# A transformer block's backward pass in head halves: column passes, a fixed TensorE order and dx in two buffers

## The chip, the cores and the metric

The kernel runs on one core of one Trainium2 chip. The metric is device time in microseconds (us) of one launch. It computes the forward pass and all gradients of one block in a single launch.

TensorE (PE) multiplies: a stationary operand is loaded into its array (the weights), a moving operand streams past, and the result lands in PSUM. VectorE (DVE), ScalarE (ACT) and GpSimd (POOL) work on rows; POOL and SyncE (SP) also issue the DMA transfers of this kernel. Each engine works through its own instruction queue in order and waits for others through semaphores.

## The reference

A block with a memory-augmented recurrent attention and a gated feed-forward layer, and the gradients of everything for a given `grad_out`:

```python
def _A_ref(x, mem0, Wq, Wk, Wv, Wo, seg_len):
    ...
    mem = mem0
    for s in range(n_seg):
        xs = x[:, s * seg_len:(s + 1) * seg_len, :].copy()
        h = jnp.concatenate([mem, xs], axis=1)
        q = jnp.einsum('btd,dhe->bhte', h, Wq)
        k = jnp.einsum('btd,dhe->bhte', h, Wk)
        v = jnp.einsum('btd,dhe->bhte', h, Wv)
        scores = jnp.einsum('bhqe,bhke->bhqk', q, k) * scale
        scores = jnp.where(mask[None, None], scores, -1000000000.0)
        p = _softmax(scores, axis=-1)
        o = jnp.einsum('bhqk,bhke->bhqe', p, v)
        o = jnp.einsum('bhte,hed->btd', o, Wo)
        mem = o[:, :M, :].copy()
        outs.append(o[:, M:, :])
    return jnp.concatenate(outs, axis=1)
...
h = x + _A_ref(_layernorm(x, axis=-1), A_mem0, A_Wq, A_Wk, A_Wv, A_Wo, A_seg_len)
h2 = h + _B_ref(_layernorm(h, axis=-1), B_w_gate, B_w_up, B_w_down)
...
_out, _vjp = jax.vjp(_f, A_x, A_mem0, A_Wq, A_Wk, A_Wv, A_Wo, B_w_gate, B_w_up, B_w_down)
_grads = _vjp(grad_out)
```

The sizes are: 2048 tokens of width 448; 16 heads of 256, so 4096 columns of q, k and v; segments of 32 tokens with 8 memory rows ahead of them, so 40 rows to a segment and 64 segments. The memory of a segment is the attention output of the first 8 rows of the segment before it. So the segments are a chain: forward from the first to the last, and backward from the last to the first, where what comes back to the memory rows of segment s is part of the output gradient of segment s-1. The feed-forward layer has an inner width of 1792. Inputs and outputs are bfloat16.

## The kernel before, in words

The launch has four stages, one after the other in time: the forward chain (0 to about 1045 us), the feed-forward layer with its gradients (1045 to 1356), the backward chain (1358 to about 2417) and the tail, which makes the weight gradients (2430 to the end).

A width of 448 is held as four chunks of 128 rows, the last half filled (`KC` = 4). The 4096 columns are 32 chunks of 128 (`MC`). On-chip memory is laid out by hand in three arenas, `arW`, `arA` and `arB`; PSUM has five banks named `psf`, two named `fx` and one named `po`.

**Order of work.** The program is written as a sequence, and a scheduler puts each engine's instructions in order by readiness and urgency: what stands under `k.prio.crit()` (the chain) goes first, and other work fills in where the chain waits. `tc.issue_after(x)` keeps an instruction behind x in its engine's order.

**Forward chain, what the change touches.** A tile of the output of earlier segments is fetched again (`fetch`, lines 604 and 605: two POOL loads) and added to the input (`residual`, L595 and the statistics after it on DVE). At segment s, with `jm` = s % 16, a fetch is issued where `jm % 3 == 1` and a residual where `jm % 3 == 0 and jm > 0`. The forward makes q and k rows by column passes (`qk_rows`, L535 and L539): the 32 new rows of a segment are the stationary operand, at four column positions of the array, and 512 columns of the weights stream past each.

**Feed-forward.** At its end each tile of the gradient `dh` is written twice to memory: in float32 (`DH`) and in bfloat16, padded from 448 to 512 columns (`DHb`, L1021 and L1022). The padding is zero.

**Backward chain.** The loop runs over s from 63 to 0; a tile t is four segments, r = s % 4 going 3, 2, 1, 0. `do_roll` holds the output gradient of the segments, transposed: per segment 32 columns of data and 8 of memory, with room for 8 segments. One segment is:

- L1151: the gradient ahead of the output projection, 128 products with a 128x128 block of `WoT_sb` as stationary operand and the 40 columns of the segment moving. Four banks of eight chunks; DVE and ACT copy them to `doT` (feature-major).
- `token_major`, L1160 and L1161: sixteen transposes and two ACT copies give `dO_sb`, token-major.
- L1169: `doT` times v, the gradient of the probabilities, 32 products into one bank `pD`. L1176, L1178, L1179 and L1181 on DVE make the gradient of the scores of all heads, written with zero blocks between head groups (`dS_bd`) by means of `P_bd`, the probabilities with zero blocks.
- `heads` (L1128 is its product): v from `dO_sb` and `P_bd`, k from q and `dS_bd`, q from k and the turned scores `dST_bd` (L1209). Sixteen products of 80 columns each; copies to `blk` (the 32 rows of a segment's data) and to `lo` (its 8 memory rows) on DVE and ACT.
- `rows_in`, L1200: 96 products over the chunks of v, k and q with `WvT_sb`, `WkT_sb` and `WqT_sb`, collected in `po`. This is the gradient of the layer's normalised rows.
- L1218 and L1219 copy it to `om`; L1222, four float32 products with a selection matrix, turns it; L1226 (DVE) writes 8 columns into `do_roll` of segment s-1. That closes the chain: L1151 of the next segment needs it. The other 24 columns of each group go to `dxT`.

Once a tile, outside of the urgent part: L1264, 96 products of the memory rows (`lo`) of the four segments with the same weights, collected in a bank `fx` (px); then L1267, L1271, the copies into `dxT`, four transposes (L1279), the layer-norm backward (`ln_bwd`) and the store of the gradient of x (`OUT1`). L1264's products are used where the chain leaves TensorE free.

On POOL's queue per segment: the load of the probabilities (L1082), two copies into `P_bd` (L1084), a copy of memory gradients (L1239) and, at set places (`later`, `stores`), the stores of q, k and v gradients (L1247, L1251). On SP's queue: the loads of v, q and k, and per tile of `xn_t` and `dh_h`.

**Tail.** `d_by_e` collects seven banks over blocks of rows, with the 64-row chunk (L1380) after every four blocks. `rows_by_d` (L1396) collects n banks over blocks, block by block, then copies and stores them. The last product group multiplies the feed-forward activations (`Zt`) by `grad_out` (`GO`, loaded at L1471) and stores the 14 results of `OUT[9]` from POOL (L1479).

## Time and profile before

| | us |
|---|---|
| median of 3 runs | 3105.77 |
| lowest and highest | 3103.6, 3115.08 |
| the profiled execution | 3105.46 |
| its span | 3103.7 |
| mean granted TensorE clock | 0.988 |

The stages, from the busy time of each engine in each stretch of the same execution (us):

| stretch | length | PE | DVE | ACT | POOL | DMA share |
|---|---|---|---|---|---|---|
| 0 to 1045, forward | 1045.0 | 936.8 | 536.0 | 435.2 | 255.8 | 0.65 |
| 1045 to 1356, feed-forward | 311.0 | 305.5 | 214.2 | 150.1 | 91.9 | 0.96 |
| 1358.4 to 2417, backward | 1058.6 | 1010.6 | 497.1 | 432.1 | 210.4 | 0.52 |
| 2430 to 3103, tail | 673.0 | 658.9 | 81.9 | 92.2 | 115.9 | 0.81 |

A line of a timeline has the start in us, the length in us, the engine, the line of the program, the operation, its output and inputs with the arrays' names, the shape, and after "x" how many such instructions were put together. In brackets stands how long the engine was idle just before, and what released it. In a line of the page's groups, the two figures after the bar are the busy time in us and the mean length of one instruction in ns, and after the second bar the idle time before them.

### The profile page before, as it was taken

How to read it: one execution, taken by the hardware profiler on the slowest of the kernel's cores; microseconds unless marked ns; L12 is line 12 of the kernel's file. 1: busy time of each engine (PE TensorE's matmuls, PEld its weight loads, DVE VectorE, ACT ScalarE, POOL GpSimd, SP SyncE). 2: the span in 40 equal slices, each digit the busy share in tenths (PEclk: the TensorE clock that was granted, in tenths of full speed). 3: DMA queues.
4: the chain of work that ended last, by engine and by line, in shares of the span. 5: the costliest groups of instructions: out<-in, count | busy, mean ns of one | idle time of the engine just before them, and what ended most of it. 6: DMA issues, size and time to landing. Idle time of an engine off the chain costs nothing.

```text
span 3103.7 us, 108341 instructions
## 1 busy us (share of the span) xinstructions
PE 2914.8 (94%) x47640; PEld 1735.5 (56%) x47650; DVE 1331.6 (43%) x3381; ACT 1112.6 (36%) x2634; POOL 674.7 (22%) x1511
## 2 busy tenths in 40 slices
PE   5899999989988999989999999999999899999998
PEld 3555555545544555666666666666666454444443
DVE  3555455455455576654444444544445101111110
ACT  2444344344444544443434344444344001111110
POOL 2222222222222222321122111221211111212111
PEclk9999999999999999999999999999999899999999
DMA  6567756756756899984455445555544999969951
GB/s 242 136 172 178 183 162 167 191 158 167 189 161 182 276 222 228 221 298 119 133 150 143 128 137 142 143 139 136 141 138 133 284 267 244 190 181 199 192 160 57
DMA packets 739084, 550.12 MB, mean 177 GB/s; under 512 B 600052, under 2 KB 634852, under 8 KB 736180
## 3 DMA queue, kind: packets, MB, share of 16 engines
q1 hardware_dynamic: 687380, 389.19, 51.5%
q0 software_dynamic: 51232, 154.00, 14.9%
q8 instruction: 374, 6.13, 0.8%
q14 instruction: 98, 0.80, 0.1%
HBM read 168.01 MB, written 234.23 MB: 130 GB/s over the span
## 4 chain that ended last, share of the span: by engine, by line
PE 72%; issue 11%; DVE 6%; DMA 5%; ACT 4%; POOL 2%; SPq 1%; ACTq 0%; POOLq 0%; DVEq 0%
PE po L1200 7%; PE psf L1151 7%; PE psf L535 6%; PE psf L652 5%; PE po L697 4%; PE psf L1375 4%; PE psf L890 4%; PE psf L1128 4%; PE psf L1396 4%; PE fx L1264 3%; PE fx L1014 3%; PE fx L464 2%; PE psf L1222 2%; DVE arA L75 2%; PE psf L549 2%
## 5 line engine op out<-in xcount | busy, mean ns | idle before, releaser
L75 DVE CAST arA<-psf 128x256 bf16<-128x256 f32 (+3 forms) x933 | 427.2, 480 | 808.6 <-PE psf L1375 275.2
L76 ACT CAST arA<-psf 128x96 bf16<-128x96 f32 (+5 forms) x915 | 352.4, 409 | 1036.6 <-PE psf L1375 261.2
L1200 PE MATMUL po<-arW,arA 128*32 128x448 bf16 x6144 | 347.3, 355 | 4.6 <-DMA arW<-Tq 3.5
L1375 PE MATMUL psf<-arW,arA 128*128 128x512 bf16 x980 | 247.1, 380 | 0.0
L1375 PEld LDWEIGHTS <-arA 128*128 128x128 bf16 x1440 | 136.0, 98 | 164.8 <-issue 13.8
L1151 PEld LDWEIGHTS <-arW 128*128 128x128 bf16 x8192 | 213.4, 96 | 25.0 <-issue 25.0
L1151 PE MATMUL psf<-arA,arW 128*128 128x40 bf16 x8192 | 217.0, 180 | 6.2 <-DVE arA L1226 5.1
L652 PE MATMUL psf<-arW,arA 128*64 128x512 bf16 x1536 | 219.0, 386 | 0.0
L1200 PEld LDWEIGHTS <-arA 128*32 128x32 bf16 x6144 | 152.0, 96 | 115.8 <-ACT arA L76 9.4
L535 PE MATMUL psf<-arW,arA 128*32 128x512 bf16 x3072 | 193.8, 385 | 12.5 <-DVE arA L738 12.5
L76 ACT CAST arB<-psf 128x64 bf16<-128x64 f32 (+3 forms) x384 | 121.8, 318 | 153.1 <-PE psf L539 109.7
L697 PE MATMUL po<-arW,arA 128*32 128x256 bf16 (+1 forms) x4096 | 144.2, 267 | 10.5 <-DVE arA L75 7.5
L890 PE MATMUL psf<-arW 128*128 128x256 bf16 (+1 forms) x1288 | 146.3, 274 | 1.3 <-DVE arA L956 0.7
L890 PEld LDWEIGHTS <-arW 128*128 128x128 bf16 (+1 forms) x1344 | 102.4, 97 | 51.4 <-issue 40.8
L1161 ACT COPY arA<-psf 128x1024 bf16<-128x1024 bf16 x128 | 123.3, 1015 | 2.2 <-PE psf L1160 0.4
L1128 PEld LDWEIGHTS <-arW 128*128 128x128 bf16 x2048 | 86.4, 99 | 61.8 <-issue 56.9
L535 PEld LDWEIGHTS <-arA 128*32 128x32 bf16 x3072 | 70.6, 97 | 90.0 <-DVE arA L738 18.1
L76 ACT COPY arA<-psf 128x512 bf16<-128x512 bf16 (+3 forms) x142 | 84.3, 594 | 99.9 <-DVE arA L75 90.3
L464 PE MATMUL fx<-arA,arW 128*128 128x64 bf16 (+1 forms) x2048 | 84.3, 196 | 32.4 <-ACT arB L76 19.2
L697 PEld LDWEIGHTS <-arA 128*32 128x32 bf16 x4096 | 95.9, 98 | 32.9 <-DVE arA L75 10.5
L1128 PE MATMUL psf<-arB,arW 128*128 128x80 bf16 x2048 | 96.8, 201 | 13.6 <-DVE arB L1181 5.2
L1436 POOL DMA_DIRECT2D out_dram<-arA x96 | 51.7, 546 | 249.7 <-DVE arA L75 246.9
(290 smaller groups left out, 4645.7 us busy)
## 6 DMA issues: line engine op xcount, KB each, us to landing
arW<-T SPq DMA_DIRECT2D x256, 128.0 KB
X_o<-arA SPq DMA_DIRECT2D x37, 512.0 KB
T<-arA SPq DMA_DIRECT2D x64, 256.0 KB
X_v<-arA POOLq DMA_DIRECT2D x32, 512.0 KB, 4.9
X_k<-arA POOLq DMA_DIRECT2D x32, 512.0 KB, 4.0
X_q<-arA POOLq DMA_DIRECT2D x32, 512.0 KB, 3.1
out_dram<-arA POOLq DMA_DIRECT2D x90, 128.0 KB, 3.5
VG<-arA SPq DMA_DIRECT2D x64, 160.0 KB
```

The source lines that it names most:

```text
L75: return nc.vector.tensor_copy(out=out, in_=in_)
L76: return nc.scalar.copy(out=out, in_=in_)
L464: nc.tensor.matmul(banks[w][:, i * 64:(i + 1) * 64], lhsT=lhsT, rhs=xr[lo:hi, kc, :], start=(kc == 0 and i == 0), stop=(kc == KC - 1), ski ...
L535: nc.tensor.matmul(banks[w][32 * q:32 * q + 32, :], lhsT=hT_roll[:, kc, sl, M:L], rhs=(Wq_sb, Wk_sb)[w][:, kc, col(q, b)], start=(kc == 0) ...
L652: nc.tensor.matmul(pV[b][64 * g:64 * g + 64, 0:512], lhsT=hT_flat[:, kc, sl * L:sl * L + 64], rhs=Wv_sb[:, kc, n * 512:(n + 1) * 512], sta ...
L697: nc.tensor.matmul(pO[32 * q:32 * q + 32, 0:w], lhsT=xblk[:, j, r * SEG:(r + 1) * SEG], rhs=Wo_sb[:, cj(j), 256 * dh:256 * dh + w], start= ...
L890: nc.tensor.matmul(ps[fp][:, f2 * 256:(f2 + 1) * 256], lhsT=Wt[lo:hi, kc, c * P:(c + 1) * P], rhs=xT[lo:hi, kc, :], start=(kc == 0 and f2 ...
L1128: nc.tensor.matmul(ps[b][:, i * 2 * L:(i + 1) * 2 * L], lhsT=lhs[:, at, :], rhs=rhs_bd[:, cl // 2, :, :].rearrange("p g n -> p (g n)"), st ...
L1151: nc.tensor.matmul(pss[b][:, jj * L:(jj + 1) * L], lhsT=WoT_sb[:, kc, c * P:(c + 1) * P], rhs=do_roll[:, kc, sl, :], start=(kc == 0), stop ...
L1200: nc.tensor.matmul(pH[32 * (j % 4):32 * (j % 4) + 32, 0:D], lhsT=blk[nm][:, j, r * SEG:(r + 1) * SEG], rhs=WT[:, cj(j), :], start=(nm == " ...
L1375: nc.tensor.matmul(pa[2 * kc + g][:, 0:w], lhsT=lhs_of(b)[:, kc * P:(kc + 1) * P], rhs=rhs_of(b, g), start=(b == 0), stop=(b == nblk - 1), ...
L1396: k.last_mm = nc.tensor.matmul(pa[i][:, 0:D], lhsT=lhs_of(b, i), rhs=rhs_of(b), start=(bi == 0), stop=(bi == len(nblk) - 1))
```

## The change

- **Forward:** the fetch needs `jm > 3` as well, the residual `jm > 5`.
- **Feed-forward:** the padding of `DHb` repeats the last 64 columns instead of zeros.
- **Backward, TensorE in program order:** every product and transpose of the stage is issued through `in_order`, behind the one before it. Nothing of the stage can be moved up into a gap any more.
- **Column passes:** `wide_pass` takes the 32 non-memory rows (the columns 8 to 40 of a segment in `do_roll`: 24 of its data and the 8 of memory) as the stationary operand at four column positions and streams the columns of Wo past: 32 products of 512 columns into two banks. These give the token-major `dO_sb` at once; `half_turned` makes `doT` from it by eight transposes in two halves. The first 8 rows of each segment of a tile are done once a tile in the same way (`rest_pass`, `dO_rest`), turned into `R`, and copied by POOL into `doT` per segment. Wo's last 64 rows are held in `WoT3`, doubled.
- **v heads:** replaced by `values`, 16 products of 160 columns: eight for the main rows and eight for the first 8 rows, with the probabilities in two new layouts. `Pq_main` is loaded per segment by four DMAs (`load_p_main`); `Pq_rest` is made by DVE (`rest_probs`) from `Pr`, which 16 DMAs load per tile (`load_p_rest`), and a mask. `P_bd` and its copies are gone.
- **Head halves:** the gradient of the scores, the k and q heads and the turned scores are done in two halves of heads, with `rows_in` between them. All copies of v are on ACT.
- **Memory-row products:** the L1264 products become `px_part` (32 at a time: q at r = 0, k at r = 3 and v at r = 2 of the next tile) and `px_end` at r = 1, each whole at the end of a segment ahead of the last copies; `dx_end` follows at r = 0. `dxT` has two buffers.
- **Tail:** the 64-row chunk can be done at the end of a group (`frees=False`); `rows_by_d` does its last four blocks accumulator by accumulator; `GO` is loaded earlier, to another place; the last stores alternate between POOL and SP.

The core of the diff:

```diff
-        if due and jm % 3 == 1:
+        if due and jm % 3 == 1 and jm > 3:
             fetch(due[0], h_t, x2_t)
...
-        if due and jm % 3 == 0 and jm > 0:
+        if due and jm % 3 == 0 and jm > 5:
             n = due.pop(0)
...
             nc.scalar.copy(out=dh_b[:, 0:D], in_=dh_t)
+            nc.scalar.copy(out=dh_b[:, D:DP], in_=dh_t[:, D - 64:D])
...
+    def in_order(op):
+        def fn(*args, **kw):
+            with tc.issue_after((pe[0] if pe else k.last_dh).ins):
+                pe[:] = [op(*args, **kw)]
+            return pe[0]
+        return fn
+    mm, tr = in_order(nc.tensor.matmul), in_order(nc.tensor.transpose)
...
-        for g in range(2):
-            pool_op = nc.gpsimd.tensor_copy(out=P_bd[64 * g:64 * g + L, :, g, :], in_=P_sb[64 * g:64 * g + L, :, :])
...
+    def load_p_main(s):
+        for q in range(4):
+            g, x = divmod(q, 2)
+            src = dr["P_all"][s, 64 * g + M:64 * g + L].rearrange("i (b x h n) -> i b x h n", b=2, x=2, n=L)
+            nc.gpsimd.dma_start(out=Pq_main[32 * q:32 * q + 32].rearrange("p (b h) q n -> p b h q n", b=2)[:, :, :, 2 * x + g, :],
+                                in_=src[:, :, x])
+
+    def load_p_rest(t):
...
+        for q in range(4):
+            g, x = divmod(q, 2)
+            for i in range(4):
+                src = dr["P_all"][4 * t + i, 64 * g:64 * g + M].rearrange("i (b x n) -> i b x n", b=2, x=2)
+                nc.gpsimd.dma_start(out=Pr[32 * q + M * i:32 * q + M * i + M].rearrange("p (b h) n -> p b (h n)", b=2), in_=src[:, :, x])
...
+    def wide_pass(banks, out, lhs_of):
+        for q in range(4):
+            for b in range(2):
+                mm(banks[b][32 * q:32 * q + 32, :], lhsT=lhs_of(KC - 1, 64 * b, 64 * b + 64),
+                   rhs=WoT3[64 * b:64 * b + 64, q * 512:(q + 1) * 512], start=True, stop=False, skip_group_check=True)
+        for b in range(2):
+            for kc in range(KC - 1):
+                for q in range(4):
+                    mm(banks[b][32 * q:32 * q + 32, :], lhsT=lhs_of(kc, 0, P), rhs=WoT_sb[:, kc, col(q, b)],
+                       start=False, stop=(kc == KC - 2), skip_group_check=True)
+        for b in range(2):
+            k.evac(out[:, b, :], banks[b][:], "vs"[b])
+
+    def half_turned(pt, src, dst, b):
+        for i in range(4):
+            tr(pt[:, (4 * b + i) * P:(4 * b + i + 1) * P], src[:, b, i * P:(i + 1) * P], ident[:, :])
+        k.evac(dst[:, 16 * b:16 * b + 16], pt[:, 512 * b:512 * b + 512].rearrange("p (c n) -> p c n", n=32), "vs"[b])
...
+    def rest_pass():
+        wide_pass([k.fx1(), k.fx1()], dO_rest, lambda kc, lo, hi: hR[lo:hi, kc].rearrange("p g i -> p (g i)"))
+
+    def rest_probs(s):
+        with tc.issue_after(k.last_ds.ins) if s < NSEG - 1 else nullcontext():
+            nc.vector.tensor_tensor(out=Pq_rest, in0=Pr.unsqueeze(2).to_broadcast([P, 4, 4, L]),
+                                in1=gmask[:, s % 4, :].unsqueeze(1).unsqueeze(3).to_broadcast([P, 4, 4, L]), op=ALU.mult)
...
+        load_p(s - 1)
+        if r == 0:
+            load_p_rest(t - 1)
+        pool_op = nc.gpsimd.tensor_copy(out=doT[:, :, 0:M], in_=R[:, :, M * r:M * r + M])
+        stores("mid", s, pool_op.ins)
...
+            wide_pass([k.ps1(), k.ps1()], dO_sb, lambda kc, lo, hi: do_roll[lo:hi, kc, sl, M:L])
...
+            half_turned(pt, dO_sb, doT[:, :, M:L], 0)
+            pv += [k.ps1() for _ in range(3)]
+            values(1)
+            half_turned(pt, dO_sb, doT[:, :, M:L], 1)
             pD = k.ps1()
...
+            grad_of_probs(0)
+            grad_of_scores(0)
+            values(0)
+            if s > 0:
+                load_p_main(s - 1)
+            grad_of_probs(1)
+            grad_of_scores(1)
...
+            if r == 0 and t < NT - 1:
+                dx_end(t + 1)
+            rows_in("v", WvT_sb, 0, 12)
+            heads("k", Q_sb, dS_bd, 0)
+            turned_scores(0)
+            rows_in("v", WvT_sb, 12, MC)
+            if r == 0 and t > 0:
+                rest_pass()
+            heads("k", Q_sb, dS_bd, 1)
+            turned_scores(1)
+            heads("q", K_sb, dST_bd, 0)
+            rows_in("k", WkT_sb, 0, 12)
+            heads("q", K_sb, dST_bd, 1)
+            rows_in("k", WkT_sb, 12, MC)
+            if r == 0 and t > 0:
+                wide_turned(dO_rest, R)
+            if s > 0:
+                rest_probs(s - 1)
             rows_in("q", WqT_sb, 0, MC)
+            if r == 0:
+                px_part(t, "q")
+            elif t < NT - 1:
+                {3: lambda: px_part(t + 1, "k"), 2: lambda: px_part(t + 1, "v"), 1: lambda: px_end(t + 1)}[r]()
...
-            for b in range(b0, min(nblk, b0 + 4)):
+            for b in range(b0, min(nblk, b0 + 4)) if frees else range(nblk) if b0 + 4 >= nblk else ():
...
-        for bi, b in enumerate(nblk):
-            for i in range(n):
-                k.last_mm = nc.tensor.matmul(pa[i][:, 0:D], lhsT=lhs_of(b, i), rhs=rhs_of(b), start=(bi == 0), stop=(bi == len(nblk) - 1))
+        m = len(nblk) - 4
+        for bi, i in [(bi, i) for bi in range(m) for i in range(n)] + [(bi, i) for i in range(n) for bi in range(m, m + 4)]:
+            b = nblk[bi]
+            k.last_mm = nc.tensor.matmul(pa[i][:, 0:D], lhsT=lhs_of(b, i), rhs=rhs_of(b), start=(bi == 0), stop=(bi == m + 3))
```

## The prediction

> **What bounds the kernel now.** I read the page's busy shares and its chain first, then the timeline of one steady backward segment, then the three places that the change touches outside it. TensorE (PE) is busy 94% of the span, and the chain lies on it for 72%:
>
> ```profile
> PE 2914.8 (94%) x47640; PEld 1735.5 (56%) x47650; DVE 1331.6 (43%) x3381; ACT 1112.6 (36%) x2634; POOL 674.7 (22%) x1511
> PE 72%; issue 11%; DVE 6%; DMA 5%; ACT 4%; POOL 2%; SPq 1%; ACTq 0%; POOLq 0%; DVEq 0%
> L1200 PE MATMUL po<-arW,arA 128*32 128x448 bf16 x6144 | 347.3, 355 | 4.6 <-DMA arW<-Tq 3.5
> L1151 PE MATMUL psf<-arA,arW 128*128 128x40 bf16 x8192 | 217.0, 180 | 6.2 <-DVE arA L1226 5.1
> ```
>
> The backward chain runs from 1358.4 to about 2417. The starts of L1151 give its segment periods: 16.04, 16.04, 16.90, 15.98 in an undisturbed tile of four (64.95), 65.2 as a mean, 24.73 and 17.15 in the first two segments. One segment on PE (start, length, idle before in brackets):
>
> ```profile
> 1708.63 3.37 PE L1151 MATMUL psf<-arA,arW 128*128 128x40 bf16 x128
> 1711.84 1.12 PE L1160 MATMUL psf<-ident,arA 128*128 128x128 bf16 x16
> 1712.89 0.69 PE L1169 MATMUL psf<-arA 128*64 128x40 bf16 x32
> 1713.61 0.46 PE L1128 MATMUL psf<-arB,arA 128*128 128x80 bf16 x8
> 1714.00 0.56 PE L1264 MATMUL fx<-arW,arA 128*32 128x448 bf16 x8
> ...
> 1723.40 0.85 PE L1222 MATMUL psf<-sel,omb 128*128 128x32 f32 x6
> 1724.18 0.55 PE L1264 MATMUL fx<-arW,arA 128*32 128x448 bf16 x5
> 1724.67 0.49 PE L1151 MATMUL psf<-arA,arW 128*128 128x40 bf16 x13
> ```
>
> No bracket shows: whenever the chain waits, L1264 (memory-row products, of low urgency) fills. Adding start-to-start times, the chain's own matmuls are 12.9 us and the 37 L1264 1.74; 1.4 of the 16.04 goes to switches and short waits. Meanwhile VectorE (DVE) has slack; its softmax gradient, with the four durations that I use:
>
> ```profile
> 1713.63 0.49 DVE L1176 SCALAR_TENSOR_TENSOR prod<-psf,arB 128x320 f32<-128x320 f32 x1 [1.91 <-PE psf L1169]
> 1714.51 0.48 DVE L1178 TENSOR_REDUCE rsum<-prod 128x8 f32<-128x320 f32 x1
> 1715.36 0.48 DVE L1179 SCALAR_TENSOR_TENSOR prod<-psf,rsum 128x320 f32<-128x320 f32 x1
> 1715.95 0.82 DVE L1181 TENSOR_TENSOR arB<-prod,arB 128x640 bf16<-128x640 f32 x1
> ```
>
> **The Trainium skill.** "TensorE: Matmul & The Clock Gate", Back-to-back issue gap, puts an issue floor of about 25 ns under small matmuls. The trace agrees: 128 L1151 start over 3.21 us, 25 ns each, for only 40 columns; so fewer, wider products pay. "TensorEngine Tiling (Array Packing)", PSUM Bottleneck, warns that after packing the PSUM copies may become the bottleneck; before, they are not (DVE 7.2, ACT 6.0 busy of the 16.04), and this is my main doubt after. "PSUM — Partial Sum Buffer", PSUM bank collisions raise a hardware error, tells to guard by bank, not by address: so two halves in one bank wait for each other's reader. No run shown here has such a wait inside a segment. The clock gate page's part on HAM says that idleness of a window drops the clock to half; after the 6.4 us stall below the granted clock reads 0.50 from 625 to 632.
>
> **The change part by part.**
>
> **Forward.** Segments 20, 36 and 52 take 19.86, 24.54, 20.54 against 15.07 for the next:
>
> ```profile
> 623.04 0.39 DVE L595 TENSOR_TENSOR arB<-arB 128x448 bf16<-128x448 bf16 x1 [6.70 <-DMA arB<-in_A_x_dram]
> ...
> 625.09 0.46 PE L628 MATMUL psf<-arA 128*40 128x40 bf16 x16 [6.41 <-ACT arA L76]
> ```
>
> L595 sits in DVE's queue ahead of copies that the chain needs. In the changed instruction order each L595 comes about three segments after its fetch. Next late is the normal period: −(4.8+9.4+5.4) = −19 us; −12 if the wait only shrinks.
>
> **Feed-forward.** Sixteen ACT copies of 64 columns (0.2 each) replace memsets, with ACT half idle there (150 busy of 311): 0; uncovered 3.
>
> **Backward, work on PE.** Out: L1151 3.21, L1160 1.05, the v heads 0.66 = 4.9 us a segment. In: the column pass, the same 24 + 8 shapes as a forward unit:
>
> ```profile
> 380.09 1.48 PE L535 MATMUL psf<-arW,arA 128*32 128x512 bf16 x24 [0.27 <-DVE arA L738]
> 381.50 0.41 PE L539 MATMUL psf<-arW,arA 64*32 64x512 bf16 x8
> 381.83 1.04 PE L535 MATMUL psf<-arW,arA 128*32 128x512 bf16 x14
> ```
>
> that is 1.74; eight transposes 0.46; sixteen values products of 160 columns, 0.08 each by estimate between the 80-column heads (41 ns) and 448-column rows (190 ns alone), 1.28; a fifth product at the end 0.15. Sum 3.6. Once a tile, the rest pass and its transposes add 2.2. Net per tile 4×(3.6−4.9)+2.2 = −3.0 us of work.
>
> **Backward, waits.** L1264 no longer fills: its products stand as whole chunks at the segment's end. I laid one segment out with the traced durations, a handover 0.05, a switch of shape 0.1: column pass 0–1.74; its bank copied by DVE (0.69), transposes to 2.17; memory-row values to 2.85; second transposes 3.09; first half of L1169's product 3.12, whose last matmul reads past its half and waits for ACT's 0.59 copy, 3.94; rest of the values 4.56. The second half writes the bank that DVE still reads: three 160-column operations (0.32 each, the forward's softmax row) end at 5.23, so PE waits 0.7. Then 5.64; v rows to 6.21; k heads and turned scores 6.83; v rows 7.78; second k heads wait for DVE's other half (7.86), done 8.66; q heads 9.00; k rows 9.57; second q heads wait for ACT's copy (9.9), 10.28; k rows 11.23; q rows 12.74; a chunk of 32 L1264 14.25; the fp32 products 15.5; DVE's copy 15.8. Period 15.85. DVE's gradient as two halves is 2×5×0.32 = 3.2 where it was 2.3, and the new rest probabilities add the 0.82 of L1181's shape.
>
> With r=1 the 32-product chunk (1.51) gives way to 8 fp32 products (1.09): 15.4. With r=0 come the rest pass 2.2, four transposes 0.65, their switches 0.5, and 0.5 as the rest pass's second product waits for DVE's layer-norm step in the same bank: 19.7. Tile: 15.85+15.85+15.4+19.7 = 66.8 against 65.2, +1.6, times 16 = +26 us. Bounds: if waits cost no more than the 1.4 of today, 14.6+14.6+14.15+17.9 = 61.25, −3.95×16 = −63; above, rival B. I take the laid-out order, since each of its waits is a fixed place in an in-order queue.
>
> **Backward, DMAs.** Per segment POOL issues four more loads, minus two copies of 0.465; per tile 16 small loads at 0.54 (L1082's row), 8.6 us. They stand ahead of the copy that puts memory rows into doT, and are moved past that copy's readers. They can start when the last rest probabilities of the tile are made (8.84 in the r=1 segment), so the copy ends at 8.84+8.6+0.54+0.5 = 18.5, which is 3.1 in the next segment; it is needed at 3.12. Taken as hidden, just. SP's queue gets the dx loads a segment later; they are needed two segments on: 0.
>
> **Start of backward.** Those 16 loads, four wide ones and the copy now precede the first segment's product (16+4)×0.54 = 10.8 us behind the last feed-forward stores, and the rest pass 2.2; some lies beside the 9 us of waits that the first segment has. I take +12 (5 to 20).
>
> **Tail.** grad_out is loaded earlier:
>
> ```profile
> 3048.19 2.03 PE L1396 MATMUL psf<-arA,arW 128*128 128x448 bf16 x5 [3.26 <-DMA arA<-in_grad_out_dram]
> 3050.01 0.95 PE L1396 MATMUL fx<-arA,arW 128*128 128x448 bf16 x2
> ```
>
> Its issue on POOL (1.2 us) waits for the last reader of the buffer it now takes, but the stores queued behind it wait for the same products: 0. The 3.26 wait goes, and 15 matmuls at 0.375 instead of 0.19: −6. Grouping the 64-row products saves switches, 0.22 a block, four or three times in eight passes: −6. The last four blocks accumulator by accumulator, and stores on two queues instead of six in a row on POOL (3.2 us): −3. Sum −15 (−8 to −16). The 13.0 us wait at 2430.7 for the X_o load stays: those stores follow the last segment as before.
>
> **The sum** is against the profiled execution, 3105.46 (span 3103.7); the median is 3105.77, so 0.3 is neglected. 3105.5−19+26+12−15 = 3109.5, rounded to 3110: no change, within 0.5% (15.5 us), about what a measurement of this kernel can tell from none.
>
> **Rivals.**
> A, faster: the waits are covered better than I laid out. For it: my gaps are single places that a few 0.1 us earlier close, and DVE would be busy only about 7.2+0.9+0.8 = 8.9 of 15 us. Against it: nothing can slip into a gap once the order is fixed. All covered gives 3110−26−63 = 3021; with most of it I put 3045.
> B, slower: POOL's queue sets the r=0 segment. Price: each issue over 0.57 us makes doT's copy late by 16 times the excess, and the gradient with it. The 0.54 of plain loads speaks against it, the 0.76 of L1340's finely cut loads for it: 16×(0.76−0.54) = 3.5 late per tile, 15 tiles, +53: 3163. It decides from 0.57 us an issue, or if the eight loads in flight land slower than 4.6 us.
> C: the forward change does not do what it says and the wait moves to a later segment: 3129.
>
> **How the numbers follow.** Forecast 0.42, with its own range 3085 to 3135 (of it 0.05 is faster by over 0.5%, 0.24 within, 0.13 slower); A 0.32, all faster; B 0.20 and C 0.06, slower. Faster 0.37, same 0.24, slower 0.39. A range of 3030 to 3165 leaves out a third of A (0.11) and under half of B (0.08).
>
> **What would show it.** Column-pass starts 15.85 apart for r=3 and 2, 15.4 for r=1, 19.7 for r=0; PE idle 0.7 before the second half of the gradient product, released by DVE; no L595 waiting for the x load and no forward segment over 17 after the first ten; a first backward segment near 37; the last product group without a wait for grad_out. If r=3 periods are 15 or less, A holds and my waits are wrong; if r=0 is over 22 with PE idle behind a POOL copy, B holds.

## The result, and the profile after

| | before | after |
|---|---|---|
| median, us | 3104.68 (3100.52 to 3115.08) | 3189.99 (3187.32 to 3199.27) |
| ratio, 95% interval | | 1.0275 (1.0242 to 1.0308) |
| profiled execution, its span | 3105.46, 3103.7 | 3199.27, 3197.5 |
| mean granted clock | 0.988 | 0.982 |

The change makes the kernel 2.75% slower, some 85 us. The forecast was 3110, with 3165 as the upper end. The profiled execution is the slowest of the four, so the sums below, which are made on the traces, come to 93.8 us and not to 85.

The page's busy shares and its chain, as they were shown of before:

```profile
PE 2889.9 (90%) x41762; PEld 1621.4 (51%) x41762; DVE 1424.2 (45%) x3608; ACT 1106.3 (35%) x2938; POOL 929.7 (29%) x1967
PE 64%; DVE 14%; issue 9%; DMA 6%; ACT 5%; POOL 2%; ACTq 0%; SPq 0%; DVEq 0%; POOLq 0%
L1045 PE MATMUL psf<-arA 128*64 128x40 bf16 (+1 forms) x2560 | 111.7, 198 | 52.3 <-DVE prod L1311 29.5
L1045 PE MATMUL psf<-arB,arW 128*128 128x80 bf16 x2048 | 116.7, 202 | 24.2 <-DVE arB L1314 16.2
```

TensorE is busy 25 us less than before (2914.8), and the span is 94 us longer: the difference lies in waiting. DVE has gone from 6% of the chain to 14%. The last two lines name two of the places. All products of the backward chain carry the line of `in_order` (L1045) now, so they are told apart by shape.

Five places divide the span: the last product of the feed-forward stage, the first and the last copy that closes a segment of the backward chain (L1226 before, L1404 after; 62 segments lie between them), and the first product of the tail.

| stretch | before | after | difference |
|---|---|---|---|
| to the last feed-forward product | 1355.36 | 1339.34 | -16.0 |
| from there to the end of the first segment | 27.71 | 49.90 | +22.2 |
| 62 segments | 1011.62 | 1092.22 | +80.6 |
| from the last closing copy to the tail | 36.05 | 29.22 | -6.8 |
| tail | 672.95 | 686.82 | +13.9 |

The forward is as forecast: no segment after the tenth is over 16.7, and its last column pass ends 21 us earlier. One steady segment on PE, with r = 2 (start, length, idle before with its releaser in brackets):

```profile
1601.40 1.82 PE L1045 MATMUL psf<-arW,arA 64*32 64x512 bf16 x32 [0.29 <-DVE arA L1404]
1603.37 0.40 PE L1045 MATMUL psf<-ident,arA 128*128 128x128 bf16 x4 [0.15 <-DVE arA L75]
...
1605.39 0.87 PE L1045 MATMUL psf<-arA 128*64 128x40 bf16 x9 [0.36 <-ACT arA L76]
1606.72 0.43 PE L1045 MATMUL psf<-arA 128*64 128x40 bf16 x16 [0.47 <-DVE prod L1311]
...
1609.86 0.46 PE L1045 MATMUL psf<-arB,arW 128*128 128x80 bf16 x8 [0.36 <-DVE arB L1314]
1610.58 0.27 PE L1045 MATMUL psf<-ident,arB 128*40 128x40 bf16 x8 [0.26 <-ACT arB L76]
...
1614.95 1.69 PE L1045 MATMUL fx<-arW,arA 128*32 128x448 bf16 x32
1616.57 1.09 PE L1045 MATMUL psf<-sel,omb 128*128 128x32 f32 x10
1617.96 1.82 PE L1045 MATMUL psf<-arW,arA 64*32 64x512 bf16 x32 [0.29 <-DVE arA L1404]
```

Where the segment of before had no bracket, this one has six, 1.9 us together, and the line at 1614.95 shows what could have filled them: the 32 memory-row products, which stand as one chunk behind the last of the waits. The period is 16.56 (before: 16.04). With r = 0 it is 20.45, and about 21.7 in 6 of the 15 tiles. A tile takes 70.1 or 71.4 where it took 65.0.

The start of the backward chain has the longest wait of the kernel:

```profile
1348.28 0.40 PE L1045 MATMUL psf<-ident,arA 128*128 128x128 bf16 x4 [0.15 <-DVE arA L75]
1374.55 1.25 PE L1045 MATMUL psf<-arB,arA 128*128 128x160 bf16 x8 [25.87 <-DVE arB L1154]
```

### The profile page after: what moved, and what is told of

Same layout as the page of the kernel before. It is cut to its first block, busy times and chain, and to the rows that moved or that the text cites. A ratio compares the mean times of both kernels' runs of the same rounds, so it can differ in the third digit from the quotient of the medians.

```text
span 3197.5 us, 97577 instructions
## 1 busy us (share of the span) xinstructions
PE 2889.9 (90%) x41762; PEld 1621.4 (51%) x41762; DVE 1424.2 (45%) x3608; ACT 1106.3 (35%) x2938; POOL 929.7 (29%) x1967
## 3 DMA queue, kind: packets, MB, share of 16 engines
q0 software_dynamic: 67424, 156.86, 15.4%
## 4 chain that ended last, share of the span: by engine, by line
PE 64%; DVE 14%; issue 9%; DMA 6%; ACT 5%; POOL 2%; ACTq 0%; SPq 0%; DVEq 0%; POOLq 0%
PE psf L1045 10%; PE psf L535 6%; PE po L1045 6%; PE psf L652 5%; PE psf L1530 5%; PE po L697 4%; PE fx L1045 4%; PE psf L888 4%; PE psf L1552 3%; DVE arA L75 3%; DVE arB L1314 3%; PE fx L1012 2%; PE fx L464 2%; ACT arA L76 2%; PE psf L549 2%
## 5 line engine op out<-in xcount | busy, mean ns | idle before, releaser
L76 ACT CAST arA<-psf 128x512 bf16<-128x512 f32 (+2 forms) x1107 | 381.8, 396 | 881.4 <-PE psf L1530 254.4
L75 DVE CAST arA<-psf 128x384 bf16<-128x384 f32 (+3 forms) x613 | 345.4, 572 | 655.0 <-PE psf L1530 268.4
L1045 PEld LDWEIGHTS <-arA 128*64 128x64 bf16 (+3 forms) x13440 | 393.7, 99 | 384.3 <-issue 75.6
L1045 PE MATMUL po<-arW,arA 128*32 128x448 bf16 x6144 | 341.0, 355 | 0.0
L1110 POOL DMA_DIRECT2D arA<-P_all x256 | 149.2, 628 | 235.4 <-PE psf L1045 220.3
L535 PE MATMUL psf<-arW,arA 128*32 128x512 bf16 x3072 | 193.7, 385 | 12.5 <-DVE arA L738 12.5
L1045 PE MATMUL psf<-arA 128*64 128x40 bf16 (+1 forms) x2560 | 111.7, 198 | 52.3 <-DVE prod L1311 29.5
L1120 POOL DMA_DIRECT2D prod<-P_all x256 | 142.6, 561 | 37.5 <-DVE arB L1154 8.9
L1045 PE MATMUL psf<-arW,arA 128*32 128x512 bf16 (+1 forms) x2048 | 124.9, 402 | 18.5 <-DVE arA L1404 18.5
L1045 PEld LDWEIGHTS <-arW 128*128 128x128 bf16 x2048 | 88.4, 99 | 101.2 <-issue 54.4
L1045 PE MATMUL psf<-arB,arW 128*128 128x80 bf16 x2048 | 116.7, 202 | 24.2 <-DVE arB L1314 16.2
L75 DVE COPY arA<-psf 128x512 bf16<-128x512 bf16 (+2 forms) x204 | 87.2, 428 | 97.8 <-PE psf L549 55.7
L535 PEld LDWEIGHTS <-arA 128*32 128x32 bf16 x3072 | 70.6, 97 | 90.0 <-DVE arA L738 18.1
```

What stands on the lines that cost most here:

```text
L75: return nc.vector.tensor_copy(out=out, in_=in_)
L76: return nc.scalar.copy(out=out, in_=in_)
L535: nc.tensor.matmul(banks[w][32 * q:32 * q + 32, :], lhsT=hT_roll[:, kc, sl, M:L], rhs=(Wq_sb, Wk_sb)[w][:, kc, col(q, b)], start=(kc == 0) ...
L1045: pe[:] = [op(*args, **kw)]
L1110: nc.gpsimd.dma_start(out=Pq_main[32 * q:32 * q + 32].rearrange("p (b h) q n -> p b h q n", b=2)[:, :, :, 2 * x + g, :], in_=src[:, :, x])
L1120: nc.gpsimd.dma_start(out=Pr[32 * q + M * i:32 * q + M * i + M].rearrange("p (b h) n -> p b (h n)", b=2), in_=src[:, :, x])
```

## The experiments

Twelve kernels; the median and the ratio to the kernel before stand first. "Tile" is the period of four steady segments. "Idle" is the time in a tile in which no product is in flight by the records, worked out from the matmul records as the median of 15 tiles; it is the measure that decided most. The median of the kernel before differs from one comparison to the next (3104.7 to 3116.1), so for small differences the ratio, which is taken within one comparison, says more than the medians of two comparisons.

| kernel | median | tile | idle | products in flight |
|---|---|---|---|---|
| before | 3105 | 65.05 | 2.3 | 62.7 |
| after | 3190 | 70.1 | 8.9 | 61.3 |
| after, free order | 3106 | 65.3 | 0.6 | 64.7 |
| after, memory-row products free | 3163 | 68.0 | 6.1 | 61.9 |
| after, fillers placed by hand | 3165 | 68.5 | 6.1 | 62.4 |
| before, fixed order | 3189 | 71.5 | 8.1 | 63.4 |

### The forward change alone

```diff
-        if due and jm % 3 == 1:
+        if due and jm % 3 == 1 and jm > 3:
...
-        if due and jm % 3 == 0 and jm > 0:
+        if due and jm % 3 == 0 and jm > 5:
```

> The kernel before with the two new conditions of the forward alone. Theory: the stalls of segments 20, 36 and 52 go and nothing else moves, 3105 - 19 = 3086. Rival (the wait moves to another segment or comes back later in the feed-forward): 3100 to 3105.

3089.57, 0.9933 (0.9911 to 0.9955). The last group of L535, the forward's column pass, starts at 1018.6 instead of 1041.5, and the steady tile is unchanged at 64.96. The gain is what the three stalls were worth, and it stays.

### The tail of before in the changed kernel

The edit puts the whole function of the tail back.

> The changed kernel with the tail of before. Theory: the changed tail saves some 13 us of TensorE time but waits 26 us at two loads that it queues behind the larger HN and GO loads, so with the old tail the stretch from the first tail product to the end is again about 673 instead of 687, and the whole about 10 lower, 3180. Rival (those waits come from the state of the memory system and not from the tail's order of loads): they appear in the old tail too, and the whole is 13 higher, 3203.

3184.9, 1.0240 (1.0206 to 1.0274). The intervals of this ratio and of the changed kernel's overlap, so the answer is read from the traces: the tail takes 676.9, ten less than 686.8. Its longest waits are 3.4 for a memory-row load and 3.1 for `grad_out`, where the changed tail has 8.0 and 15.9. In the changed kernel POOL's queue at the first of these two places was (start, length, what is issued):

```profile
2636.06 1.17 POOL L1621 DMA_DIRECT2D arW<-HN  x1 [0.16 <-issue]
2637.22 0.55 POOL L1566 DMA_DIRECT2D out_dram<-arA  x1
2637.77 0.76 POOL L1495 DMA_DIRECT2D arA<-M_v  x1
2638.52 0.76 POOL L1495 DMA_DIRECT2D arB<-M_v  x1
```

and TensorE then waited for the small load:

```profile
2655.76 1.01 PE L1509 MATMUL ph<-ident,arB 128*128 128x128 bf16 x8 [7.96 <-DVE arW L75]
...
2960.17 1.01 PE L1509 MATMUL ph<-ident,arB 128*128 128x128 bf16 x8 [15.90 <-DVE arW L75]
```

The order is what counts here: the 1.8 MB load of HN comes first, the smaller memory-row load `M_v` (0.5 MB) behind it. It lands 16.8 us after its issue; before, where it was issued first, it took 8.2. All the traces agree: in the five kernels that issue this load ahead of HN it takes 6.7 to 9.9, in the nine that issue it behind, 16.2 to 17.1. At the second place the moved `grad_out` load stands ahead in the same way (issued at 2935.0, the small load at 2936.2 and landed 22.8 later).

### One copy from DVE to ACT

```diff
-                    k.evac(of(blk[nm])[...], v[...], "vvs"[i])
+                    k.evac(of(blk[nm])[...], v[...], "s" if nm == "k" and b == 0 else "vvs"[i])
```

> The changed kernel with one PSUM copy a segment (first k heads, 384 columns) on ACT instead of DVE. Theory (DVE's in-order queue sets the pace: this copy stands between the two halves of the second softmax gradient, and TensorE waits 0.36 for the latter): segments of 16.56 become about 16.1, 64 x 0.45 = 29 us less, 3161. Rival (the fixed TensorE order with its handovers sets it, and the wait moves to ACT or to the turned scores): under 0.1 a segment, 3185.

3175.49, 1.0203 (1.0163 to 1.0244). Segments of 16.23, a third of a microsecond less; a tile of 68.9. That is 15 us less by the medians and 22 by the ratios, and lies between the two expectations. The wait is real, but it is one of several and the next takes over part of it. DVE in the changed kernel shows it:

```profile
1624.66 0.32 DVE L1311 SCALAR_TENSOR_TENSOR prod<-psf,rsum 128x160 f32<-128x160 f32 x1
1624.90 0.55 DVE L75 CAST arA<-psf 128x384 bf16<-128x384 f32 x1
1625.37 0.99 DVE L1314 TENSOR_TENSOR arB<-prod,arB 40x160 bf16<-40x160 f32 x2
```

The copy L75 serves rows that are needed later; L1314 behind it is what TensorE waits for at 1626.42 (0.36).

### The first rest loads from SP

```diff
-    load_p_rest(NT - 1)
+    load_p_rest(NT - 1, nc.sync)
```

> The changed kernel with the sixteen first loads of rest probabilities issued from SP instead of POOL. Theory (on POOL they wait one by one for the feed-forward stores eight transfers back, so the 25.9 us wait at the start of the backward chain is one of queueing): the wait falls to under 8 us and the median by about 18, 3172. Rival (the loads themselves are slow, or wait for the buffer that they fill): the wait stays near 25, 3190.

3187.59, 1.0245 (1.0207 to 1.0284): no gain that can be told. The wait is 21.5 us instead of 25.9. It is not POOL's queue alone. SP's sixteen issues take 23.8 us as well: seven are out by 1345.7, and the eighth comes at 1355.2.

```profile
1337.50 23.80 SPq L1121 DMA_DIRECT2D prod<-P_all  x16
```

### TensorE free to be ordered

```diff
-    mm, tr = in_order(nc.tensor.matmul), in_order(nc.tensor.transpose)
+    mm, tr = nc.tensor.matmul, nc.tensor.transpose
```

> The changed kernel without the fixed TensorE order: products may fill gaps by readiness and urgency. Theory (waits in the DVE and ACT queues, not the TensorE order, make the segments longer; but px chunks can now fill them): 0.5 to 1 us a segment less, 3130 to 3160. Rival (the new scheme needs the order: without it long rest and px products get in the way of the chain): 3190 or more.

3105.94, 0.9992 (0.9974 to 1.0011). This is more than either theory expected: the whole loss of 84 us goes with one line, although the waits at the start (24.3 us) and in the tail stay. The same places as in the segment above, in the free order:

```profile
1602.17 0.43 PE L1300 MATMUL psf<-arA 128*64 128x40 bf16 x15
1602.53 0.45 PE L1279 MATMUL psf<-arA 128*128 128x160 bf16 x4
1602.96 0.21 PE L1300 MATMUL psf<-arA 128*64 128x40 bf16 x1
1603.10 0.45 PE L1279 MATMUL psf<-arA 128*128 128x160 bf16 x4
1603.48 0.37 PE L1203 MATMUL fx<-arW,arA 128*32 128x448 bf16 x3
1603.49 0.92 PE L1357 MATMUL po<-arW,arA 128*32 128x448 bf16 x9
1604.34 0.43 PE L1300 MATMUL psf<-arA 128*64 128x40 bf16 x16
```

The sixteenth product of the first half (L1300 x1) and the second half (x16) wait as long as before for ACT and DVE, but values (L1279), memory-row products (L1203) and v rows (L1357) lie in those times. No bracket is left in this stretch. Periods are 15.33, 15.33, 16.55 and 18.05 for r = 3, 2, 1, 0.

### Only the memory-row products free

```diff
-            mm(px[32 * (j % 4):32 * (j % 4) + 32, 0:D], lhsT=lo[:, j, :], ...
+            nc.tensor.matmul(px[32 * (j % 4):32 * (j % 4) + 32, 0:D], lhsT=lo[:, j, :], ...
```

(and the same for the products and transposes of `px_end` and `dx_end`.)

> The changed kernel with the chain still in the fixed order, but the memory-row products (px_part, px_end, dx_end) free to be placed anywhere. Theory (what the fixed order costs is filling: the chain's 2 us of waits a segment stay empty since the px products stand behind them): periods of 16.56 become 15.3 to 15.6, nearly those of the wholly free order, 3110 to 3125. Rival (the order among the chain's own products costs as much): only half of the 84 us comes back, 3145 or more.

3163.07, 1.0157 (1.0123 to 1.0191): 27 of the 84 us by the medians, some 37 by the ratios. My theory falls and the rival holds. The memory-row products go into the first waits of a segment (in the one that starts at 1646.6, with r = 3, 19 of them into two waits, while the next two, 0.23 and 0.26, stay empty), and in the segment with r = 1 there are none left. The chain's own products, which may not pass each other here, are the larger store of fillers.

### Free order and three repairs

Free order, the copy on ACT, the first rest loads on SP, and the `grad_out` load moved to the last attention group (`if hi == 5`).

> The changed kernel with free TensorE order, the first k copy on ACT, the first rest loads on SP and the grad_out load moved behind the last attention group. Theory: 3106 for the free order, -18 at the start, -8 at the tail (the 16 us wait goes, the 8 us one at the HN load stays), and at most -5 for the copy since TensorE is full in the free order: 3075 to 3082. Rival (the copy matters as in the fixed order): another -20, 3055 to 3060.

3118.07, 1.0022 (1.0005 to 1.0040): nothing was gained. Four things changed at once, so the traces have to tell them apart. The tile is 65.85, 0.6 longer than in the free order alone, and the copy on ACT is the only one of the repairs that touches it. The start still waits 19.9 (24.3 in the free order), and the tail takes 691.6 where it took 676.5, with waits of 8.2, 7.1, 7.9 and 3.5 for memory-row loads, although `grad_out` no longer stands ahead of most of them.

### The kernel before in a fixed order

The edit adds `in_order` to the backward chain of before and issues its products and transposes through it.

> The kernel before with the backward chain's TensorE work in program order, nothing else changed. Theory (a fixed order leaves the chain's waits empty whatever the products are): the memory-row products stand bare behind each tile's last segment, 6.3 us a tile, and the segments keep some 14.5 + 1.5: 3105 + 16 x (6.3 - 1.6 to 3) = 3160 to 3180. Rival (only the new scheme with its small groups and split softmax suffers): within 20 of before, under 3125.

3189.37, 1.0240 (1.0205 to 1.0276). Against the first median of before, 3105, that is 84 us lost, as much as the changed kernel's fixed order costs; by the ratio it is 75, the theory's upper figure. The old scheme in the same kind of segment:

```profile
1608.11 0.46 PE L1046 MATMUL psf<-arB,arA 128*128 128x80 bf16 x8 [0.46 <-ACT arA L1171]
...
1610.51 0.73 PE L1046 MATMUL psf<-arB,arW 128*128 128x80 bf16 x16 [0.31 <-DVE arB L1191]
...
1612.93 0.73 PE L1046 MATMUL psf<-arB,arW 128*128 128x80 bf16 x16 [0.26 <-ACT arB L76]
...
1616.35 1.29 PE L1046 MATMUL psf<-sel,omb 128*128 128x32 f32 x8 [0.50 <-DVE omb L1228]
1617.92 4.06 PE L1046 MATMUL psf<-arA,arW 128*128 128x40 bf16 x128 [0.28 <-DVE arA L1236]
...
1650.92 1.70 PE L1046 MATMUL fx<-arW,arB 128*32 128x448 bf16 x32
1652.44 3.20 PE L1046 MATMUL fx<-arW,arA 128*32 128x448 bf16 x64
```

It has waits of its own, of about the same sum (1.8 us). The memory-row products, the last two lines, stand bare behind each tile and make one period of every tile 22.45. The line at 1617.92 shows a second cost: 4.06 for a group that takes 3.35 elsewhere, since the granted clock was 0.50 from 1619.1 to 1622.5. In 26 of the last 59 segments the clock fell in this way, and they take about 16.7 where the others of their kind take 15.69, some 26 us in all; the mean clock of this run is 0.974. In the same part of the chain the changed kernel has 6 such falls, of 1.3 us each, and the kernel before and the changed one in free order have none. So the two losses are of like size, and not made of the same parts.

### Before, with the forward change and the tail in order

```diff
-            nc.gpsimd.dma_start(out=HN[:, 0:NT, :], in_=dr["HN"]...)
+            with tc.issue_after(k.last_fetch.ins):
+                nc.gpsimd.dma_start(out=HN[:, 0:NT, :], in_=dr["HN"]...)
```

`k.last_fetch` is the last memory-row load issued; the `grad_out` load is moved to the last attention group and kept in the same way.

> The kernel before with the forward change and the changed tail, but with the HN load kept behind the memory-row loads in POOL's order, and the grad_out load behind the last of them. Theory (the changed tail's products are some 9 us shorter once no large load stands ahead of the small ones): the stretch from the first tail product to the end is about 660 instead of 669, the whole 3089 - 9 = 3080. Rival (the memory-row loads are late in the shorter tail anyway, since a block of products now leaves them less time): 3086 to 3092.

3080.91, 0.9906 (0.9880 to 0.9932). The tail takes 657.1 with no wait over 1.2 us after its first product, where the forward change alone has 669.3. That it gains over the forward change is read from these two traces; the two ratios alone don't settle it, since their intervals overlap. The memory-row loads now stand ahead:

```profile
2546.64 0.76 POOL L1340 DMA_DIRECT2D arA<-M_v  x1 [0.40 <-ACT arA L1347]
2547.59 0.76 POOL L1340 DMA_DIRECT2D arB<-M_v  x1 [0.18 <-issue]
2548.34 1.16 POOL L1467 DMA_DIRECT2D arW<-HN  x1
```

This version beats both kernels.

### A fixed order with the fillers in the gaps

```diff
+                            if b == 0 and (h, g, dc) == (3, 1, 1):
+                                values(0, (0,))
...
-            values(0)
+            values(0, (1,))
...
+            px_piece(8)
             grad_of_probs(1)
...
+            px_piece(8)
             heads("k", Q_sb, dS_bd, 1)
+            px_piece(6)
             turned_scores(1)
...
+            px_piece(2)
             heads("q", K_sb, dST_bd, 1)
```

> The changed kernel, still in a fixed TensorE order, with that order edited at the places where TensorE waited for r = 3 and 2: half of the values ahead of the sixteenth product, and the 32 memory-row products cut to 8, 8, 6 and 2 at the four waits and 8 at the end. Theory (the order is not bad for being fixed, but for where the fillers stand): periods of 16.56 become 15.5 for r = 3 and 2, 16.3 for r = 1 and 20.2 for r = 0, 3 us a tile, 3142. Rival (DVE's and ACT's chain is what counts, and fillers only shift it): under 0.5 a segment, 3170 or more.

3165.17, 1.0184 (1.0141 to 1.0227): 25 us come back by the medians, 28 by the ratios. Periods of 15.88, 15.88, 16.28 and 20.45. Placing helps by 0.7 where there are fillers, as the theory has it, though less than it said: the wait ahead of the second half of the gradient is 0.25 where it was 0.47, not gone, and with r = 1, where half of the values now stands earlier and no memory-row products are left, it grows to 0.74. r = 0, which has no fillers, is unchanged.

### Without the first rest loads

```diff
-    load_p_rest(NT - 1)
+    nc.gpsimd.memset(Pr, 0.0)
```

> The changed kernel without the sixteen first loads of rest probabilities: the buffer is zeroed instead, so the first 8 rows' part in the v gradient of the last tile is left out. Theory (the 25.9 us wait at the start is of these loads, which stand behind stores that take 14 to 18 us to land): the wait falls to under 5, with some of it coming back as waits for the weights, and the first segment's end is 12 to 18 earlier, 3175. Rival (the weights' loads hold the start anyway): waits of the same sum elsewhere, 3188.

3171.86, 1.0190 (1.0162 to 1.0219). The wait is gone, and one for the weights comes up in its place, as in the kernel before (3.47 there):

```profile
1359.89 3.18 PE L1045 MATMUL po<-arW,arA 128*32 128x448 bf16 x32 [4.53 <-DMA arW<-Tq]
```

From the last feed-forward product to the end of the first segment it is 28.9 us instead of 49.9. So those loads cost the start 21 us in the traces, nearly all of what it lost. In the changed kernel the median of them lands 2.1 us after its issue, but the first eight were each held on POOL until a store had landed, and those stores took 9 to 18 us, with the DMA engines 98% busy from 1300 to 1340. Three of the eight:

```profile
1351.98 0.55 POOL L1120 DMA_DIRECT2D prod<-P_all  x1 [1.52 <-DMA DGP<-arA]
1356.13 0.54 POOL L1120 DMA_DIRECT2D prod<-P_all  x1 [3.60 <-DMA DU<-arA]
1360.92 0.55 POOL L1120 DMA_DIRECT2D prod<-P_all  x1 [4.25 <-DMA DH<-dh_t]
```

The first five loads also land late, 15.8 to 4.6 us after their issue, all between 1364.6 and 1365.5. Taken with the run on SP: either queue was held, POOL's behind the stores, SP's by the pause after its seventh issue, right after the weights' loads. What held SP's, and the first five loads here, I did not separate further.

### Free order with whole heads

The two halves of the gradient, of k, of the turned scores and of q are each done in one go, in free order.

> The changed kernel with free TensorE order and whole heads: one gradient of the scores for all heads, then k, the turned scores and q each in one go. Theory (in the free order TensorE has no idle time left, and the price of the halves is the changes between small groups of products, some 0.09 each and 122 a tile where the kernel before has 74): with about 30 changes less a tile goes from 65.3 to 62.5, 3106 - 44 = 3062. Rival (the halves are needed: without them TensorE waits for one long softmax gradient of 2.4 us and nothing is left to fill it): a tile of 65 or more with idle time ahead of the k heads, 3106 or more.

3121.84, 1.0029 (1.0014 to 1.0043). A tile of 65.8 with 1.3 us idle. Neither expectation holds. The long gradient is covered well, so the halves are hardly needed in the free order, but nothing is gained by leaving them: a tile is 0.5 longer than with them. My price of 0.09 for each change between groups stays untested, since the order that came out has nearly as many changes (116 a tile by line and shape, where the free order with halves has 121): the scheduler cuts the long groups again to fill waits.

## Why the prediction was wrong

**Backward, waits: this is the step that failed.** It gave a tile of 66.8, +26 us in all; the 62 segments took 80.6 more. Its places were right. The waits for ACT, for the bank that DVE still reads and for DVE's second half are all where the text put them, up to 1606.7 within 0.1 us of the laid-out times. The sizes were not. The second k heads start 8.46 into the segment instead of 7.91, since DVE's order puts a copy of 0.55 ahead of the last part of the gradient; the turned scores then wait for ACT as well, and the period is 16.56 instead of 15.85. With r = 1 it is 16.56 instead of 15.4: I took 0.4 off for the shorter chunk, but ACT's second half of the closing copy then stands behind the dx copies and TensorE waits 0.31 more, and 0.17 more for ACT ahead of the second q heads. With r = 0 it is 20.45 instead of 19.7. In 7 of 15 tiles 1.3 us come on top at a lower granted clock (the seventh is the first tile, 20.0 where four other kernels in a fixed order have 18.7). The 0.66 of the first line below is a mean: the clock was 0.50 from 1564.3 to 1567.7 and 1.00 around it (the columns are the stretch, its length, busy time of PE, PEld, DVE, ACT and POOL with counts, the clock, DMA share and GB/s):

```profile
1563.00:1568.00 5.00, 4.76 (x63) 2.94 (x63) 1.30 (x3) 1.08 (x3) 2.46 (x5) 0.66 0.02 2
1634.50:1639.50 5.00, 4.34 (x72) 2.75 (x73) 1.80 (x5) 1.84 (x5) 3.25 (x7) 1.00 0.16 27
```

**What the forecast weighed least was the fixed order itself.** It named that nothing can fill a gap, and took the resulting waits for a price to be set against less work. The two runs with `in_order` removed and added show what this order is worth in either scheme: 3190 to 3106 here and 3105 to 3189 in the kernel before by the medians, 2.8% and 2.4% of the time by the ratios. In the table, the fixed order has 8 to 9 us idle in a tile, the free ones 0.6 and 2.3. It is the order as it was written that costs this: with fillers put into some of its gaps by hand, nearly a third of the loss came back.

**Backward, work.** Said: 3.0 us less a tile. Measured, in the fixed order: products in flight for 61.3 instead of 62.7, so 1.4 less; against the old scheme in a fixed order, 63.4, it is 2.1, with a part of the 63.4 due to the lower clock there. In the free order they are in flight for 64.7. They are cut into more and smaller groups there, which may be the reason; no run shows it. That the column passes have fewer instructions (1116 a tile, 1484 before) brings nothing here: with every gap filled, a tile takes 65.3 in the new scheme and 65.05 in the old.

**Forward.** Said -19; alone it gives 3089.6 against a median of 3107.8 of before in the same comparison, -18. Right. (Its three terms add up to 19.6, so -20 would have been the rounded figure.)

**Start.** Said +12 by the number of issues on POOL (10.8 us). Measured +22.2. The term was mis-sized: an issue took 0.54 to 0.59 as said, but between them POOL waited up to 4.25 us for stores to land, which the text named ("behind the last feed-forward stores") and did not price. Without the sixteen loads the stretch is 28.9, 1.2 longer than before.

**Tail.** Said -15. The stretch is 13.9 longer, or 7.1 with the 6.8 gained ahead of it, which the text had at nothing: the X_o wait is 3.0 instead of 13.0, after a longer end of the chain. The products' gain was right in size: without its two long waits of 24 us the tail would by this estimate be 663, ten less than before, and it is 657 in the version with the loads in order. What I had at nothing, the earlier grad_out load, was the failure: I asked which buffer it waits for, and not which smaller load stands behind it.

**POOL's queue at r = 0 (rival B)** did not happen. The copy to doT was put ahead of the sixteen loads (1625.30, the loads from 1627.86), and those take 0.561 each and are needed a segment later. Of the times named, B's 3163 is the nearest to the measured 3190, by accident.

**C** did not happen either. **A** named the right question, how well the waits are covered, and had it the wrong way round. Nor was its bound within reach: with the waits covered, in the free order, a tile takes 65.3 and not 61.25. One reading behind its bound was off: the segment of before has 32 memory-row products and not 37, since five of those counted start ahead of it, and so 1.6 us and not 1.4 went to switches and short waits. This moves nothing else.

Of the sections of the Trainium skill, "TensorEngine Tiling (Array Packing)", PSUM Bottleneck, warns that the copies out of PSUM may become the bottleneck, and five of the six waits of a segment (0.29, 0.15, 0.36, 0.47 and 0.26) are for such a copy or for another reader of PSUM. But the fixed order is what made them a cost: with the same copies and a free order, a tile has 0.6 us idle. The rule of "PSUM — Partial Sum Buffer", PSUM bank collisions raise a hardware error, to guard by bank showed itself as the wait of 0.47 for DVE's third gradient operation. The 25 ns a product that the trace gave for L1151 led me to count instructions, which were not what limited a tile.

**The clock in the r = 0 segments.** The trace shows what tells the slow ones from the others. All changes of the granted clock in it lie on one grid with a step of 3.413 us: the low stretches of the steady tiles begin at 1564.3, 1704.3, 1776.0, 1847.6, 1919.3 and 2131.0, which are 41, 21, 21, 21 and 62 steps apart. The clock fell where a step came between 0.35 us before and 1.11 us after the start of the segment's column pass, and in no other r = 0 segment. This holds for all 84 such segments after the first tile, 33 of them with a fall, in the traces of six kernels in a fixed order: the changed one and those with the old tail, the copy on ACT, the loads on SP, the fillers placed by hand and the first rest loads left out. The segments have the same gaps, so it is their place on the grid that decides.

**What stays open:** what in the 3.4 us ahead of such a step counts as too little work (products are in flight for 2.8 us of the stretch from 1560.9 to 1564.3, and stretches with less keep the clock); how much a change between small groups costs; and why some of the tail's memory-row loads are late with no large load of POOL ahead of them, in the free order with three repairs (15.0 at 2673.7) and without the first rest loads (15.8 at 2725.8).

## What to carry to other kernels

Before fixing an engine's order by hand, list each wait of its chain and what fills it today; the filler includes the chain's own later products, not only the background work. Fewer instructions brought nothing here, where the gaps were filled anyway. A load that is moved up must be judged by what then stands behind it in its queue, the smaller transfers above all.

## What the hardware showed that I had not expected

- A load of 0.5 MB that lands in 8.2 us when it is issued ahead of a 1.8 MB load lands in 16.8 behind it, and TensorE waited 8.0 for that.
- Sixteen small loads, of which the median lands in 2.1 us, took 23 us to issue, since each of the first eight was held until an earlier store had landed.
- The granted clock fell to 0.50 for 3.4 us after stretches in which no gap was over 0.4 us, and whether it fell depended on where a segment lay on a grid of 3.41 us. The mean clock of the kernel before fell from 0.988 to 0.974 with the fixed order.
